# A fused transformer block: Q and K of the first two tiles read from the loaded weights on 32-column tiles, with the first stage re-ordered

## The chip, the cores and the metric

The kernel runs on one core of a Trainium2 chip. The metric is the device time of one execution in microseconds (us), taken over several runs. Five engines matter: TensorE (PE; PEld is its weight load), VectorE (DVE), ScalarE (ACT), GpSimd (POOL) and SyncE (SP), which issues the transfers. Each runs its own program in order, and they meet through semaphores.

## The reference

One block with adaptive layer norm over S = 2048 tokens, D = 448 channels, H = 16 heads of 28, F = 1792. Cut to what is computed:

```
mod = silu(c) @ w_mod                  # six rows of 448: sa, ca, ga, sb, cb, gb
h = layernorm(x) * (1 + ca) + sa
q, k, v = heads of h @ wqkv            # 448 -> 3 * 448
for each position s and head: keys at s - 2*w, w = 0..7, those >= 0
    o = softmax(q.k / sqrt(28)) @ v
x = x + ga * (o @ wo)
h = layernorm(x) * (1 + cb) + sb
x = x + gb * (gelu(h @ w1 + b1) @ w2 + b2)
```

Inputs and output are bf16.

## The kernel before

The dilation of 2 splits the tokens into two interleaved sub-sequences of 1024. A tile is 128 positions of both, so there are 8 tiles of 256 tokens. Attention runs in 9 batches of 114 positions: scores `lt` (L738), exp and a mask multiply into `et`, denominators `pd` (L760), outputs `po` (L771, 128 small matmuls of 64x57 a batch), a division, and the output projection `pw` (L803). The MLP (L548 and L554 for W1, L883 for W2) is done in two phases, each after its share of the batches, so that the chain of attention overlaps with W1 and W2 matmuls.

**Two ways to Q and K.** Tiles 0 and 1 take the short way: the normalised tokens `zy` are transposed on PE (`ptr`, L535), scaled and shifted into `hT`, and Q and K are made feature-major. Heads have 28 features but sit on 32 partitions of `qT` and `kT`, so the loaded weights `wqk_st` (128 rows) and `wqr_st` (the last 64 rows, kept twice, on both halves of the partitions) are first copied into `Wqk` and `Wqr` with every head spread to 32 columns: ten copies, lines L439 to L450. The matmuls (`pq`, L562, L548, L554) then take 128 spread columns as stationary weights and 128x256 of `hT` as moving data. Tiles 2 to 7 take the long way: `zy` goes through a DMA transpose `zT` (L527), DVE writes `hT` (L502), PE makes Q and K token-major with `hT` as the stationary side (L548, L554), and they come to `qT` and `kT` through ACT and DMA transposes (L631).

**What sets the order.** All work is recorded as numbered tasks; a written-out table `ORDER` gives the order in which they are emitted, an engine letter where a task has a choice of engine, and "+12@55" where 12 filler matmuls on zeros are put ahead (into the accumulator of task 55). `SLOTS` gives each buffer's place. The tables thus fix every engine's program. All transfers are issued by SP in table order; in the built program each waits also for the eighth transfer before it on SP.

**The first stage.** x and the weights of the first modulation (`wm_st`, `wm_r`), `wqk_st`, `wqr_st` and `Wv` are loaded; DVE takes layer-norm statistics (L456, L458), POOL or ACT turn them into `rs_all` (L469 on POOL), DVE writes `zy` (L478), whose tail columns are copied on POOL (L490). POOL also builds the attention mask (L280 to L289) and zero pads. silu(c) is made on DVE, L396, and copied to 32 columns on ACT, L398. The later modulation matrix `wmod` is loaded in four pieces (L362) for the matmuls of L641.

Of the kernel before, what the change touches and what calls it, by code (L numbers as in the profile page):

```python
# [10 lines left out]
BF16 = mybir.dt.bfloat16  # L11
# [55 lines left out]
487 401 490 454 403 402 436 453 455 370 444 404 434 371:D 456 372 491 457 488 405 459 493 458 460 445 492 435 494 461  # L67
# [3 lines left out]
513 515:D 547 599 516 564 602 481 568 569 570 604 571 603 546 605 572 548 606 573 628 607 608 574 549 635 575 550 609  # L71
612 636 577 630 578 637 610 629 576 640 579 638 581 639 611 613 580 582 583 641 631 586 633 587 651 584 614 632 585
616 588 615 617 642 618 648 646 647 621 654 634 619 645 622 652 620 656 649 623 644 658 643 625 624 650 589 590 626
591:A 664 655 627 653 439 657 592 659 556 665 662 663 674 666 660 661 669 667 675 668 678 676 679 677 686 672 673 671
687 681 670 680 690 691 694 697 693 682 688 692 685 695 683 689 701 684 698 696 709 699 710 702 711 712 705 700 703
706 704 707 708
# [77 lines left out]
def kernel(  # L154
# [41 lines left out]
    Wqk = cst.tile([128, KT - 1, 2, H, HP], BF16, name="Wqk")  # L196
    Wqr = cst.tile([128, 2, H // 2, HP], BF16, name="Wqr")
# [25 lines left out]
    silu_bf = cst.tile([128, KT], BF16, name="silu_bf")  # L223
# [11 lines left out]
    wqk_st = sb("hm", [128, KT - 1, 2 * D + HP - DH], BF16, "wqk_st")  # L235
    wqr_st = sb("h2", [128, 2 * D + HP - DH], BF16, "wqr_st")
# [9 lines left out]
    def dconst(us, fn, writes):  # L246
        early.append(add("DVE", us, fn, writes=writes, after=[one], name="const " + writes[0]))
# [22 lines left out]
    dconst(0.06, lambda: nc.vector.memset(neg_half[:], -0.5), ["neg_half"])  # L270
# [46 lines left out]
    def load(fn, us, writes, bufs=(), reads=(), fills=()):  # L317
        queue.append(add("SP", 0.5, fn, reads=reads, writes=writes, bufs=bufs, fills=fills, after=queue[-1:] if len(queue) < 4 else queue[3:4], xfer=us,
                         name="load " + writes[0]))
# [8 lines left out]
    def load_rest(a):  # L328
        load(lambda a=a: nc.sync.dma_start(out=wqr_st.t[KS * a:KS * a + KS, :], in_=A_wqkv[(KT - 1) * 128:D, 0:2 * D + HP - DH]),
             0.5, [f"wr{a}"], bufs=[wqr_st])  # L330

    def load_wv():
        load(lambda: nc.sync.dma_start(out=Wv[:, 0:KT - 1, :], in_=rows128(A_wqkv[0:(KT - 1) * 128, 2 * D:3 * D])), 1.15, ["wv"])
        for a in range(2):
            load(lambda a=a: nc.sync.dma_start(out=Wv[KS * a:KS * a + KS, KT - 1, :], in_=A_wqkv[(KT - 1) * 128:D, 2 * D:3 * D]),
                 0.2, [f"wvr{a}"])
# [17 lines left out]
    load_rest(0)  # L354
    load_rest(1)
    load_x(2, 4)
# [30 lines left out]
    def c_cols():  # L387
# [8 lines left out]
    add("DVE", 0.08, lambda: nc.vector.tensor_tensor(out=silu_bf[:], in0=e_c[:], in1=psc.t[:, 0, 0:128 * KT:128], op=ALU.mult),  # L396
        reads=["e_c"], bufs=[psc], writes=["silu"], name="silu")
    add("ACT", 0.18, lambda: nc.scalar.copy(out=silu_bc[:], in_=silu_bf[:].unsqueeze(2).to_broadcast([128, KT, HP])),  # L398
        reads=["silu"], writes=["silu_bc"], name="silu_bc")
# [32 lines left out]
    def spread(half):  # L432
        def heads(ap, h):
            return bass.AP(ap.tensor, ap.offset, [*ap.ap[:-1], [DH, h], [1, HP]])

        for ks in [[k] for k in range(KT - 1)]:
            k0, n = ks[0], len(ks)
            dst, src = (lambda k0=k0, n=n: Wqk[:, k0:k0 + n, half]), (lambda k0=k0, n=n: heads(wqk_st.t[:, k0:k0 + n, half * D:half * D + D], H))
            add("DVE", 0.06 + 0.18 * n, lambda dst=dst, src=src: nc.vector.tensor_copy(out=dst(), in_=src()), reads=[f"wqk{k}" for k in ks],  # L439
                bufs=[wqk_st], writes=[f"W{half}{k}" for k in ks], port=True, name="spread",  # L440
                alt={"ACT": (0.13 + 0.43 * n, lambda dst=dst, src=src: nc.scalar.copy(out=dst(), in_=src())),
                     "POOL": (0.1 + 0.5 * n, lambda dst=dst, src=src: nc.gpsimd.tensor_copy(out=dst(), in_=src()))})

        for a in range(2):
            rows, c0 = slice(KS * a, KS * a + KS), half * D + a * D // 2
            src = lambda rows=rows, c0=c0: heads(wqr_st.t[rows, c0:c0 + D // 2], H // 2)
            add("DVE", 0.22, lambda rows=rows, src=src: nc.vector.tensor_copy(out=Wqr[rows, half], in_=src()), reads=[f"wr{a}"],
                bufs=[wqr_st], writes=[f"Wr{half}{a}"], port=True, name="spread r",
                alt={"ACT": (0.33, lambda rows=rows, src=src: nc.scalar.copy(out=Wqr[rows, half], in_=src())),
                     "POOL": (0.4, lambda rows=rows, src=src: nc.gpsimd.tensor_copy(out=Wqr[rows, half], in_=src()))})  # L450


    exps, lt_mms, w1_mms, gelus = [], [], [], []

# [508 lines left out]
```

## Time and profile before

| quantity | value |
|---|---|
| median of 3 runs | 168.64 us (167.93 to 169.38) |
| the profiled execution: its own time | 169.75 us |
| its span on the core | 168.1 us |
| TensorE clock granted | 1.0 |
| PE busy | 161.5 us, 96% of the span, 2126 matmuls |
| DVE, ACT, POOL busy | 115.8, 102.7, 47.7 us |
| moved by DMA | 18.78 MB in 35574 packets |
| chain that ended last | PE 81%, DMA 10%, the rest 2% or less each |

The span is what the core's records cover; the execution's own time is 1.65 us longer. The median of the plain runs lies 1.1 us below the profiled execution's time. "Chain" is the work that ended last, followed back from the end. Up to about 34 us the chain runs through loads, DVE, POOL and transposes; from there on it is nearly all PE.

### The profile page before, as it was taken

The numbers are of one execution on the slowest core, as the hardware profiler recorded it, in microseconds if no ns is written. First come the engines' busy times: TensorE is split into PE (matmuls) and PEld (weight loads), VectorE is DVE, ScalarE is ACT, GpSimd is POOL, SyncE is SP. The second block draws the span as 40 slices with busy tenths as digits, with TensorE's granted clock in tenths as the row PEclk, the third lists the DMA queues.
The fourth block names the chain that finished last, engine by engine and source line by source line (L and its number), as shares of the span: only waits on it lengthen the run. The fifth ranks groups of instructions, "written<-read, shape, count | busy, mean of one in ns | idle before, by whom it ended". The sixth has DMA issues, their size and how long they took to land.

```text
span 168.1 us, 4962 instructions
## 1 busy us (share of the span) xinstructions
PE 161.5 (96%) x2126; PEld 83.4 (50%) x2126; DVE 115.8 (69%) x271; ACT 102.7 (61%) x142; POOL 47.7 (28%) x76
## 2 busy tenths in 40 slices
PE   7989989999997999999999999999999999999992
PEld 4768544345544544435565444556434455444562
DVE  6869899879899689998738877474798930400032
ACT  3368987779489954759866376956627730097300
POOL 4135252300361201269300113820003870007200
PEclk9999999999999999999999999999999999999999
DMA  5999989799997999910091000008110027110003
GB/s 153 325 335 297 168 265 134 152 201 170 221 200 182 236 150 236 169 35 0 4 139 46 4 0 0 4 0 97 35 55 0 0 43 195 49 60 0 0 0 109
DMA packets 35574, 18.78 MB, mean 112 GB/s; under 512 B 28508, under 2 KB 34593, under 8 KB 35553
## 3 DMA queue, kind: packets, MB, share of 16 engines
q1 hardware_dynamic: 35548, 18.47, 53.0%
q8 instruction: 16, 0.26, 0.7%
q14 instruction: 6, 0.04, 0.1%
q10 hardware_dynamic: 4, 0.00, 0.0%
HBM read 9.81 MB, written 1.84 MB: 69 GB/s over the span
## 4 chain that ended last, share of the span: by engine, by line
PE 81%; DMA 10%; DVE 2%; POOL 2%; issue 1%; SPq 1%; ACT 1%; POOLq 0%; DVEq 0%
PE p L883 26%; PE p L548 22%; PE pw L803 7%; PE pq L548 6%; PE p L554 4%; DMA x_all<-in_A_x_dram 4%; PE po L771 3%; PE lt L738 3%; PE pv L706 3%; PE pv L548 3%; DMA wm_st<-in_w_mod_dram 3%; DMA zT<-zy 2%; DMA kT<-zy 2%; PE pq L554 1%; PE pd L760 1%
## 5 line engine op out<-in xcount | busy, mean ns | idle before, releaser
L864 ACT ACTIVATE hm<-p,b_col 128x512 bf16<-128x512 f32 x56 | 33.9, 692 | 29.9 <-PE p L554 27.3
L883 PE MATMUL p<-w_s,hm 128*128 128x448 bf16 (+1 forms) x238 | 44.1, 342 | 0.0
L548 PE MATMUL p<-yT,w_s 128*128 128x512 bf16 x168 | 38.1, 379 | 0.0
L469 POOL TENSOR_TENSOR rs_all<-mvs,neg_half 128x2 f32<-128x2 f32 x22 | 16.7, 766 | 57.9 <-DVE mvs L458 57.8
L883 PEld LDWEIGHTS <-hm 128*128 128x128 bf16 x238 | 22.7, 98 | 19.2 <-issue 0.8
L889 DVE TENSOR_TENSOR x_all<-p,x1p 128x896 bf16<-128x896 f32 (+2 forms) x10 | 8.9, 902 | 25.9 <-PE p L883 25.9
L548 PEld LDWEIGHTS <-w_s 128*128 128x128 bf16 x168 | 15.8, 98 | 20.9 <-issue 2.9
L456 DVE BATCH_NORM_STATS2 stt<-x_all 128x6 f32<-128x448 bf16 x32 | 18.7, 610 | 1.2 <-DMA x_all<-in_A_x_dram 1.0
L745 ACT ACTIVATE et<-lt 128x928 bf16<-128x928 f32 x18 | 16.1, 947 | 5.3 <-PE lt L738 5.1
L841 POOL TENSOR_TENSOR x1p<-x_all,gbb_bc 128x448 f32<-128x448 bf16 x16 | 17.8, 1134 | 0.0
L548 PE MATMUL pq<-wqk_st,hT 128*128 128x448 bf16 x72 | 15.2, 354 | 0.6 <-DVE hT L502 0.5
L788 DVE TENSOR_TENSOR qT<-po,den 128x912 bf16<-128x912 f32 x9 | 9.9, 1104 | 7.0 <-ACT den L782 5.6
L751 DVE TENSOR_TENSOR et<-et,mask 128x928 bf16<-128x928 bf16 x18 | 11.6, 672 | 2.4 <-ACT et L745 2.4
L803 PE MATMUL pw<-wo_s,qT 128*128 128x448 bf16 x64 | 13.2, 353 | 0.0
L780 ACT ACTIVATE den<-pd 128x928 f32<-128x928 f32 x9 | 8.5, 940 | 5.8 <-PE pd L760 5.7
L819 DVE TENSOR_TENSOR h<-h,mod_bc 128x896 bf16<-128x896 bf16 x16 | 11.1, 709 | 0.3
L548 PEld LDWEIGHTS <-hT 128*128 128x128 bf16 x72 | 6.4, 98 | 7.7 <-issue 1.3
L628 ACT CAST zy<-pq 128x896 bf16<-128x896 f32 x10 | 9.0, 906 | 2.0 <-PE pq L554 1.9
L810 DVE TENSOR_TENSOR x_all<-pw,x_all 128x896 bf16<-128x896 f32 x8 | 8.7, 1088 | 1.7 <-PE pw L803 1.5
L782 ACT ACTIVATE den<-den,den_bias 128x928 f32<-128x928 f32 x9 | 9.6, 1072 | 0.2
L478 DVE TENSOR_SCALAR zy<-h,mvs,rs_all 128x448 bf16<-128x448 bf16 x16 | 6.6, 456 | 4.4 <-POOL rs_all L469 4.3
L456 DVE BATCH_NORM_STATS2 stt<-h 128x6 f32<-128x448 bf16 x16 | 9.4, 613 | 0.2
(115 smaller groups left out, 183.4 us busy)
## 6 DMA issues: line engine op xcount, KB each, us to landing
w_s<-in_B_w_dram SPq DMA_DIRECT2D x7, 224.0 KB, 4.2
out_dram<-x_all SPq DMA_DIRECT2D x7, 224.0 KB, 2.2
x_all<-in_A_x_dram SPq DMA_DIRECT2D x3, 448.0 KB, 6.0
wmod<-in_w_mod_dram SPq DMA_DIRECT2D x3, 448.0 KB, 7.0
w_s<-in_B_w_dram SPq DMA_DIRECT2D x3, 448.0 KB
wqk_st<-in_A_wqkv_dram SPq DMA_DIRECT2D x3, 225.0 KB
wm_st<-in_w_mod_dram SPq DMA_DIRECT2D x1, 672.0 KB
x_all<-in_A_x_dram SPq DMA_DIRECT2D x2, 224.0 KB, 2.6
```

The source lines that it names most:

```text
L456: add("DVE", 0.53, lambda: nc.vector.bn_stats(out=stt[:, w, b, 0:6], in_=src()), reads=reads, bufs=bufs, after=early if w == b == 0 else ( ...
L469: ways = {"POOL": (0.55 + 0.17 * n, lambda: nc.gpsimd.tensor_tensor(out=r, in0=v, in1=neg_half[:, 0:n], op=ALU.pow))}
L548: nc.tensor.matmul(out(), lhsT=lhs(kt, slice(0, 128)), rhs=rhs(kt, slice(0, 128)), start=first and kt == 0, stop=not first and kt == KT - 2)
L745: exps.append(add("ACT", 0.83, lambda half=half, lt=lt: nc.scalar.activation(out=et.t[:, 2 * half:2 * half + 2].rearrange("p r m c -> p r ...
L751: nc.vector.tensor_tensor(out=ev, in0=ev, in1=mask[:], op=ALU.mult)
L782: exps.append(add("ACT", 0.96, lambda: nc.scalar.activation(out=den.t[:], in_=den.t[:], func=ACT.Exp, scale=-1.0, bias=den_bias[:]), bufs= ...
L788: nc.vector.tensor_tensor(out=qT[:, :, LEAD + q00:LEAD + q00 + 2 * WQ], in0=po.t[:, :, 0:NS * 4 * WQ].rearrange("p j (m c) -> p m j c", c=WQ),
L803: nc.tensor.matmul(pw.t[:, s, 0:D], lhsT=qT[:, KT * s + ft, LEAD + 128 * p:LEAD + 128 * p + 128], rhs=wo_s[:, ft, :], start=(ft == 0), sto ...
L819: add("DVE", 0.55, lambda vec=vec, op=op: nc.vector.tensor_tensor(out=h2.t[:], in0=h2.t[:], in1=vec.unsqueeze(1).to_broadcast([128, NS, D] ...
L841: add("POOL", 1.0, lambda n=n: nc.gpsimd.tensor_tensor(out=x1p.t[:, n, :], in0=xn(p, n), in1=gbb2_bc[:], op=ALU.add), reads=[f"x{p}", "gbb ...
L864: gelus.append(add("ACT", 0.585, lambda f=f, a=a, p1=p1s[g]: nc.scalar.activation(out=hm.t[:, f].rearrange("p n c -> p (n c)"), in_=p1.t[: ...
L883: nc.tensor.matmul(p2.t[:, n, 0:c1 - c0], lhsT=hm.t[:, f, n, q * 128:(q + 1) * 128], rhs=w2_s[:, f, c0:c1], start=(f == parts[0][0]), stop ...
```

## The change

1. **Q and K of tiles 0 and 1.** A matmul now takes 32 columns of `wqk_st` or `wqr_st` (28 of a head and 4 of the next) as stationary weights and writes 32 partitions of the accumulator; the four column groups are filled by four matmuls in turn. The 64 matmuls on weights 128 columns wide become 256 on weights 32 wide (L565 of the changed file), with the same 128x256 of moving data each. The ten spread copies and `Wqk`, `Wqr` are gone. `ORDER` asks for 25 filler matmuls where it asked for 35. In all PE has 2308 matmuls for 2126.
2. **Loads.** `wqk_st` rows are 896 elements for 900; `wm_r`, `wqr_st` and the rest of `Wv` come in one transfer each onto 128 partitions where two on 64 did; tiles 2 and 3 of x come in a transfer each. The four pad columns of `wqk_st` and `wqr_st` are set to zero on DVE.
3. **silu** is written to 32 columns by one DVE operation; the ACT copy is gone.
4. **Order.** Tables, task numbers and SLOTS are new. From the scores matmul that starts at 33.71 us in the profile before, each engine's program is the same, instruction by instruction; only the first stage differs, and on PE everything after it stands 182 matmuls (364 instructions) later in the program.

On SP, in the first stage, `x_all`, `Wv` and `wmod` are loads and `zT` the transposes of tiles 2 and 3. Before:

```order
L339 DMA x_all<-in_A_x_dram 128x2x896 x2
L333 DMA Wv<-in_A_wqkv_dram 128x3x448
L335 DMA Wv<-in_A_wqkv_dram 64x448
L339 DMA x_all<-in_A_x_dram 128x2x896
L362 DMA wmod_274<-in_w_mod_dram 128x1792
L335 DMA Wv<-in_A_wqkv_dram 64x448
L362 DMA wmod_274<-in_w_mod_dram 64x1792
L527 DMA_TRANSPOSE zT<-zy_97 128x8x128
L527 DMA_TRANSPOSE zT<-zy_98 128x8x128
```

The same place in the changed kernel:

```order
L342 DMA x_all<-in_A_x_dram 128x896 x2
L338 DMA Wv<-in_A_wqkv_dram 128x3x448
L339 DMA Wv<-in_A_wqkv_dram 128x1x448
L342 DMA x_all<-in_A_x_dram 128x2x896 x2
L508 DMA_TRANSPOSE zT<-zy_96 128x8x128
L508 DMA_TRANSPOSE zT<-zy_97 128x8x128
L363 DMA wmod_581<-in_w_mod_dram 128x1792
L363 DMA wmod_581<-in_w_mod_dram 64x1792
```

The two `wmod` loads moved from ahead of the two transposes to behind them.

On POOL, in the first stage, `rs_all` is the inverse standard deviation and `zy` the copy of its tail columns. Before:

```order
L442 COPY Wqk<-wqk_st 128x512
L450 COPY Wqr<-wqr_st 64x256
L469 TENSOR_TENSOR rs_all<-mvs,neg_half 128x2
L450 COPY Wqr<-wqr_st 64x256
L469 TENSOR_TENSOR rs_all<-mvs,neg_half 128x2 x2
L280 MEMSET mask_90 128x58
L283 AFFINE_SELECT mask_90<-mask_90 64x58
L285 AFFINE_SELECT mask_90<-mask_90 64x58
L283 AFFINE_SELECT mask_90<-mask_90 64x58
L285 AFFINE_SELECT mask_90<-mask_90 64x58
L490 COPY zy_98<-zy_98 128x2x64
```

The same place in the changed kernel:

```order
L281 MEMSET mask_88 128x58
L284 AFFINE_SELECT mask_88<-mask_88 64x58
L286 AFFINE_SELECT mask_88<-mask_88 64x58
L284 AFFINE_SELECT mask_88<-mask_88 64x58
L286 AFFINE_SELECT mask_88<-mask_88 64x58
L290 COPY mask<-mask_88 128x928
L450 TENSOR_TENSOR rs_all<-mvs,neg_half 128x2 x4
L471 COPY zy_100<-zy_100 128x2x64
```

The copies of weights are gone, and the mask is built ahead of the first `rs_all`.

On PE, the end of the 128 outputs `po` of one attention batch and the matmuls behind them. Before, the first of these rows is the 1357th of the program:

```order
L771 LDWEIGHTS vb_115
L771 MATMUL po<-et,vb_115 32x57
L554 LDWEIGHTS hT
L554 MATMUL pq<-wqr_st,hT 128x448
L554 LDWEIGHTS hT
L554 MATMUL pq<-wqr_st,hT 128x448
L548 LDWEIGHTS hT
L548 MATMUL pq<-wqk_st,hT 128x448
```

In the changed kernel the first of them is the 1721st:

```order
L740 LDWEIGHTS vb_112
L740 MATMUL po<-et,vb_112 32x57
L535 LDWEIGHTS hT
L535 MATMUL pq<-wqr_st,hT 128x448
L535 LDWEIGHTS hT
L535 MATMUL pq<-wqr_st,hT 128x448
L529 LDWEIGHTS hT
L529 MATMUL pq<-wqk_st,hT 128x448
```

The instructions are the same and stand 364 places later.

The diff, cut to its core:

```diff
 ORDER = """
-3 14 17 0 1 15 5 9 10 18 11 16 13 19 20 2 6 24 21 73 55+12@55 26 12 71 25 56 72 74 57 75 22 58 77 23 59 60 27 62 61 76
+3 14 17 0 1 15 5 9 10 18 11 16 13 19 2 6 70 53+8@53 23 7 20 21 54 8 24 68 22 55 56 71 69 57 25 72 74 26 59 60+10@60 73
...
     def load_qk(kt):
-        load(lambda: nc.sync.dma_start(out=wqk_st.t[:, kt, :], in_=A_wqkv[kt * 128:kt * 128 + 128, 0:2 * D + HP - DH]), 0.62, [f"wqk{kt}"],
+        load(lambda: nc.sync.dma_start(out=wqk_st.t[:, kt, 0:2 * D], in_=A_wqkv[kt * 128:kt * 128 + 128, 0:2 * D]), 0.62, [f"wqk{kt}"],
              bufs=[wqk_st])
...
+    def both(src, n):
+
+        return bass.AP(src.tensor, src.offset, [[n, 2], *src.ap])
+
+    def load_rest():
+        load(lambda: nc.sync.dma_start(out=wqr_st.t[:, 0:2 * D], in_=both(A_wqkv[(KT - 1) * 128:D, 0:2 * D], 0)),
+             0.5, ["wr0", "wr1"], bufs=[wqr_st])
...
-    add("ACT", 0.18, lambda: nc.scalar.copy(out=silu_bc[:], in_=silu_bf[:].unsqueeze(2).to_broadcast([128, KT, HP])),
-        reads=["silu"], writes=["silu_bc"], name="silu_bc")
+    add("DVE", 0.2, lambda: nc.vector.tensor_tensor(
+        out=silu_bc[:], in0=e_c[:].unsqueeze(2).to_broadcast([128, KT, HP]),
+        in1=psc.t[:, 0, :].rearrange("p (k n) -> p k n", n=128)[:, :, 0:HP], op=ALU.mult),
+        reads=["e_c"], bufs=[psc], writes=["silu_bc"], name="silu_bc")
...
-    def spread(half):
...
+                        rest, first = kt == KT - 1, not state
+                        state.append(kt)
+                        for r, a in [(r, a) for r in range(4) for a in range(2)] if rest else [(r, a) for a in range(2) for r in range(4)]:
+                            rows = slice(KS * a, KS * a + KS) if rest else slice(0, 128)
+                            w = wqr_st.t[rows] if rest else wqk_st.t[:, kt]
+                            d0 = half * D + DH * (4 * (i + 2 * a) + r)
+                            nc.tensor.matmul(pq.t[HP * r:HP * r + HP, a, NS * 128 * i:NS * 128 * (i + 1)], lhsT=w[:, d0:d0 + HP],
+                                             rhs=hT[rows, NS * kt:NS * kt + NS, c0:c0 + 128], start=first, stop=len(state) == KT,
+                                             tile_position=(rows.start, HP * r))
```

More of the change, by code (lines that the diff above doesn't have):

```diff
@@ L244, with dconst @@
     early = []
-    def dconst(us, fn, writes):
-        early.append(add("DVE", us, fn, writes=writes, after=[one], name="const " + writes[0]))
+    def dconst(us, fn, writes, bufs=()):
+        early.append(add("DVE", us, fn, writes=writes, bufs=bufs, after=[one], name="const " + writes[0]))
     def const(us, fn, writes, reads=()):
@@ L317, in load @@
     def load(fn, us, writes, bufs=(), reads=(), fills=()):
-        queue.append(add("SP", 0.5, fn, reads=reads, writes=writes, bufs=bufs, fills=fills, after=queue[-1:] if len(queue) < 4 else queue[3:4], xfer=us,
+        queue.append(add("SP", 0.5, fn, reads=reads, writes=writes, bufs=bufs, fills=fills, after=queue[-1:] if len(queue) < 3 else queue[2:3], xfer=us,
                          name="load " + writes[0]))
@@ L324, in load_qk @@
     def load_qk(kt):
[L325 removed]
+        load(lambda: nc.sync.dma_start(out=wqk_st.t[:, kt, 0:2 * D], in_=A_wqkv[kt * 128:kt * 128 + 128, 0:2 * D]), 0.62, [f"wqk{kt}"],
              bufs=[wqk_st])
[L328 to L330 removed]
+    def both(src, n):
[3 more added lines that the diff above has]
+             0.5, ["wr0", "wr1"], bufs=[wqr_st])
     def load_wv():
         load(lambda: nc.sync.dma_start(out=Wv[:, 0:KT - 1, :], in_=rows128(A_wqkv[0:(KT - 1) * 128, 2 * D:3 * D])), 1.15, ["wv"])
[L334 to L336 removed]
+        load(lambda: nc.sync.dma_start(out=Wv[:, KT - 1, :], in_=both(A_wqkv[(KT - 1) * 128:D, 2 * D:3 * D], 0)), 0.3, ["wvr0", "wvr1"])
     def load_x(p0, p1):
@@ L347 @@
          2.1, ["wm0"], bufs=[wm_st])
-    for v in range(2):
-        load(lambda v=v: nc.sync.dma_start(out=wm_r.t[KS * v:KS * v + KS, :], in_=w_mod[(KT - 1) * 128:D, v * D:v * D + D]),
-             0.25, [f"wmr{v}"], bufs=[wm_r])
+    load(lambda: nc.sync.dma_start(out=wm_r.t[:], in_=both(w_mod[(KT - 1) * 128:D, 0:D], D)), 0.4, ["wmr0", "wmr1"], bufs=[wm_r])
     for kt in range(KT - 1):
@@ L353 @@
     load_x(1, 2)
-    load_rest(0)
-    load_rest(1)
-    load_x(2, 4)
+    load_rest()
+    load_x(2, 3)
+    load_x(3, 4)
     load_wv()
@@ L430 @@
     modulation()
-    def spread(half):
[L433 to L450, printed above, removed]
     exps, lt_mms, w1_mms, gelus = [], [], [], []
     def stats(src, w, b, reads, bufs=()):
-        add("DVE", 0.53, lambda: nc.vector.bn_stats(out=stt[:, w, b, 0:6], in_=src()), reads=reads, bufs=bufs, after=early if w == b == 0 else (),
+        add("DVE", 0.53, lambda: nc.vector.bn_stats(out=stt[:, w, b, 0:6], in_=src()), reads=reads, bufs=bufs,
             writes=[f"st{w}_{b}"], name="stats")
@@ L541, in front_ln, with summed @@
             affine(u, lambda kt: ptr[kt % 2].t[:, :, kt // 2], [(ptr[0], q) for q in range(np_)], ptr, True)
-    def summed(items, slot, reads, bufs, fills, name, after=(), split=None):
+    def summed(items, slot, reads, bufs, fills, name, after=()):
         def full(first):
@@ L555, in rest @@
                                  tile_position=(rows.start, 0))
-        us = 3.5 * len(items) * slot + 0.1
-        if split:
-            for kt in range(KT - 1):
-                def piece(kt=kt):
-                    for out, lhs, rhs in items:
-                        nc.tensor.matmul(out(), lhsT=lhs(kt, slice(0, 128)), rhs=rhs(kt, slice(0, 128)), start=kt == 0, stop=False)
-                add("PE", len(items) * slot, piece, reads=reads + [f"W{name[-2]}{kt}", f"h{kt}_0"], bufs=bufs, fills=fills, after=after,
-                    instr=2 * len(items), name=f"{name}f{kt}")
-            return [add("PE", 0.5 * len(items) * slot, lambda: rest(False), reads=reads + split, bufs=bufs, fills=fills, mode="64x128",
-                       instr=2 * len(items), name=name + "r")]
         both = dict(reads=reads, bufs=bufs, joins=fills, after=after)
@@ L576, in summed, with front_qk @@
                 add("PE", 0.5 * len(items) * slot, lambda: part(rest), instr=2 * len(items), mode="64x128", name=name + "r", **both)]
[L578 to L582 removed]
+    def front_qk(p):
+        c0 = LEAD + 128 * p
         for half in range(2):
[L585 to L611 removed]
@@ new lines, in front_qk, with piece @@
+            pq = psum("pq")
+            done = []
+            for i in range(2):
+                state = []
+                def piece(kts, i=i, half=half, pq=pq, state=state):
+                    for kt in kts:
+                        rest, first = kt == KT - 1, not state
[7 more added lines that the diff above has]
+                                             tile_position=(rows.start, HP * r))
+                mine = []
+                for kts in [[kt] for kt in range(KT - 1)] if p == i == 0 else [list(range(KT - 1))]:
+                    mine.append(add("PE", 0.22 * len(kts), lambda kts=kts, piece=piece: piece(kts), reads=["wqpad"] + [f"wqk{kt}" for kt in kts] + [f"h{kt}_{p}" for kt in kts],
+                                    bufs=[pq, wqk_st], joins=[pq], after=done, mode="128x32", instr=16 * len(kts),
+                                    name=f"qk{p}_{half}{'ab'[i]}f" + (str(kts[0]) if len(kts) == 1 else "")))
+                mine.append(add("PE", 0.11, lambda piece=piece: piece([KT - 1]), reads=["wqpad", "wr0", "wr1", f"h{KT - 1}_{p}"],
+                                bufs=[pq, wqr_st], joins=[pq], after=done, mode="64x32", instr=16, name=f"qk{p}_{half}{'ab'[i]}r"))
+                done = mine
@@ L614, in natural_qk @@
+            dst = (kT if half else qT)[:, :, c0:c0 + 128].rearrange("p (s f) c -> p s f c", s=NS)
+            src = lambda pq=pq: pq.t[:].rearrange("p a (i s c) -> p s (a i) c", i=2, s=NS)
+            add("ACT", 0.91, lambda dst=dst, src=src: nc.scalar.copy(out=dst, in_=src()), bufs=[pq], writes=[f"{'qk'[half]}{ft}_{p}" for ft in range(4)],
+                alt={"DVE": (1.14, lambda dst=dst, src=src: nc.vector.tensor_copy(out=dst, in_=src()))}, name="evac_qk")
     def natural_qk(p):
@@ L897 @@
         front_ln(u, True)
-        if k == 0 and u[0] not in NATURAL:
-            spread(0)
-            spread(1)
         if u[0] in NATURAL:
@@ L903 @@
         else:
-            front_qk(u)
+            front_qk(u[0])
     b1_cols()
```

83 lines of the change are left out of this document (28 added, 55 removed), and 21 rows, old and new, of tables (ORDER, SLOTS).

## The prediction

> **What bounds the kernel now.** I read the head of the page first, for how much of the span PE is at work.
>
> ```profile
> span 168.1 us, 4962 instructions
> PE 161.5 (96%) x2126; PEld 83.4 (50%) x2126; DVE 115.8 (69%) x271; ACT 102.7 (61%) x142; POOL 47.7 (28%) x76
> q8 instruction: 16, 0.26, 0.7%
> ```
>
> PE has work in 96% of the span, so a stage can save only what PE idles there, or PE's own work. The third line is the queue that brings instructions: 0.26 MB in 16 packets, 16 KB each. PE's 2126 matmuls and as many weight loads make 4252 instructions, and 4252 / 16 = 266; what each packet holds comes out below. Next, the waits of PE, with total, count and longest:
>
> ```profile
> PE lt L738 <- issue: 0.8, 1, 0.8
> PE pq L548 <- DVE hT L502: 0.5, 1, 0.5
> PE pq L562 <- DVE Wqk L439: 0.4, 1, 0.4
> PE lt L738 <- DMA kT<-zy: 0.4, 1, 0.4
> ```
>
> Three of the four belong to the first stage, 1.3 us together. The longest, "issue", is waited for by no semaphore. The chain of waits shows where these lie (start, length, what):
>
> ```profile
> 6.32 6.00 DMA x_all<-in_A_x_dram
> ...
> 15.87 0.07 POOL mask L280
> ...
> 17.17 0.29 POOL zy L490
> ...
> 17.56 3.38 DMA zT<-zy
> ...
> 22.79 2.25 PE pq L548 x11
> ...
> 30.57 3.09 DMA kT<-zy
> ...
> 33.71 0.70 PE lt L738 x62
> ...
> 50.57 0.48 PE lt L738 x43
> 51.05 0.85 issue
> 51.90 0.34 PE lt L738 x18
> ...
> 57.52 0.02 issue
> 57.55 0.62 PE po L771 x58
> ```
>
> Up to 22.79 us the chain runs from a load of x over statistics, POOL and the transpose to the first token-major Q and K. From there PE hardly stops: the two "issue" pieces fall in the middle of one run of like matmuls. I counted PE's matmuls up to each of them, and up to four other moments (window, length, busy time and count of PE, PEld, DVE, ACT, POOL, clock, DMA share, GB/s):
>
> ```profile
> 0.00:11.60 11.60, 9.82 (x95) 7.17 (x96) 9.21 (x50) 5.01 (x11) 3.98 (x18) 1.00 0.84 264
> 0.00:37.69 37.69, 34.96 (x551) 20.73 (x559) 31.45 (x106) 26.33 (x39) 12.18 (x33) 1.00 0.92 226
> 0.00:38.20 38.20, 35.47 (x610) 21.19 (x610) 31.69 (x106) 26.84 (x40) 12.18 (x33) 1.00 0.91 224
> 0.00:45.03 45.03, 42.30 (x735) 24.85 (x738) 37.87 (x115) 31.50 (x45) 13.22 (x34) 1.00 0.94 220
> 0.00:51.50 51.50, 48.33 (x861) 27.80 (x862) 44.16 (x131) 37.05 (x52) 16.02 (x37) 1.00 0.98 214
> 0.00:57.54 57.54, 53.95 (x989) 30.61 (x990) 49.50 (x144) 42.64 (x59) 17.47 (x39) 1.00 1.01 217
> 0.00:85.32 85.32, 81.72 (x1316) 43.76 (x1324) 73.92 (x193) 61.08 (x83) 28.22 (x51) 1.00 0.87 181
> 0.00:85.95 85.95, 82.35 (x1390) 44.34 (x1390) 73.92 (x193) 61.38 (x84) 28.22 (x51) 1.00 0.87 181
> ```
>
> The pieces stand at matmuls 861 and 989: 128 matmuls and 128 weight loads apart, which is 256 instructions. Sixteen KB for 256 instructions is 64 bytes each. So I read the pieces as ends of an instruction block, with ends at every 128th matmul: ..., 93, 221, ..., 605, 733, 861, 989, ..., 1373, 1501. Views of the DMA queues over three short windows, 39.6 to 40.7, 49.44 to 50.67 and 87.5 to 88.46 us, hold one packet of that queue each:
>
> ```profile
> q8 instruction: 1, 0.02, 5.4%
> q8 instruction: 1, 0.02, 6.1%
> q8 instruction: 1, 0.02, 6.0%
> ```
>
> A packet that fills one of 16 engines' time would read 6.2%, so each took nearly its whole window. Matmul 605 is passed just before 38.20 (x610), 733 just before 45.03 (x735), 1373 between 85.32 and 85.95: each packet follows one passage, and the packet of 49.44 came after PE had entered the block before the stall at 51.05. A block's successor is fetched when the block is entered. From entry to landing that is about 2.5 us (38.2 to 40.7), 2.6 (85.85 to 88.46) and 5.6 (45.0 to 50.67). In the third case PE went on only at 51.90, 1.2 us after the packet. A block that PE runs through faster than this cannot have its successor ready.
>
> **The shift of the blocks.** PE's program after 33.71 us is the same, 182 matmuls later. So a block end of the changed kernel at matmul 861 is old matmul 679, and the block from 733 to 861 holds the old 551 to 679. The rows say what that is: 551 matmuls are begun at 37.69 us, and then come these:
>
> ```profile
> 37.70 1.44 PE L771 MATMUL po<-et,vb 64*32 64x57 bf16 x128
> 85.33 1.39 PE L771 MATMUL po<-et,vb 64*32 64x57 bf16 x128
> ```
>
> The block is exactly the 128 `po`, gone through in 1.4 us; in the old program the end at 605 cuts them in two. A later block, from 1501 to 1629, is old 1319 to 1447: the second row, with 1316 begun at 85.32. Each must then wait for its successor. With 2.55 us from entry to landing (the two cases nearest in place) and 0.6 for the step from packet to work, halfway between none and the 1.2 measured once, that is 2.55 + 0.6 - 1.4 = 1.75 us at about 39, and 1.75 again at about 87. Without the step each is 1.15, with all of it 2.35. PE has nothing to hide it with: no other wait of it after 33.71 us stands in the list but the one at 51.05. That one goes, since the block that ends in it moves: -0.85. What takes its place as late there? Nothing in the list of waits. Sum behind the first stage: 3.5 - 0.85 = +2.65, with bounds 2.3 - 0.85 = +1.45 and 4.7 - 0.85 = +3.85.
>
> [...]
>
> **The first stage.** Its end is the `lt` at 33.71. From 22.79 to there PE's only idle is 0.4 for `kT`, and the transfer of `kT` itself is issued behind work of that same stretch, so I take the whole stretch to move with the start of 22.79. That start has two conditions.
>
> The transposes: POOL's mask work stands between the `rs_all` and the `zy` copy, 15.87 to 17.17, 1.3 us of the chain, and it now lies ahead of all `rs_all`, when POOL has room (3.98 us of work in the first 11.60). The load at 6.32 is split, and its first half has a shorter transfer. The two loads of `wmod` that stood ahead of the transposes on SP stand behind them. So `zT` should land at least 1.3 us sooner, at about 19.6 instead of 20.94 (17.56 + 3.38). The queue allows it:
>
> ```profile
> 16.00:17.00 1.00, 1.00 (x40) 0.88 (x33) 1.00 (x4) 0.65 (x1) 0.81 (x4) 1.00 0.36 97
> ```
>
> Its DMA share fell to 0.36 while POOL was at the mask. What is put behind the transposes, `wmod`, is used by L641 at 27 us (row below), so it has room.
>
> PE: it was free 0.5 us ahead of 22.79, that is at 22.25. Its wait of 0.4 for `Wqk` goes with the copies, and ten fillers of the size of an old QK matmul (0.12, below) go (-1.2), of which I count half, since some stood in waits. The price of the new matmuls comes from these rows, with mean durations in ns behind the bar in the first two:
>
> ```profile
> L641 PE MATMUL pb<-wmod,silu_bc 128*32 128x448 bf16 (+1 forms) x16 | 1.1, 357 | 0.0
> L641 PEld LDWEIGHTS <-silu_bc 128*32 128x32 bf16 (+1 forms) x16 | 0.3, 94 | 0.8 <-issue 0.7
> 27.03 1.05 PE L641 MATMUL pb<-wmod,silu_bc 128*32 128x448 bf16 x16
> 75.21 3.19 PE L883 MATMUL p<-w_s,hm 128*128 128x448 bf16 x16
> 12.58 2.79 PE L548 MATMUL pq<-hT,Wqk 128*128 128x256 bf16 x24
> 15.31 0.61 PE L554 MATMUL pq<-hT,Wqr 64*128 64x256 bf16 x8
> ```
>
> Sixteen matmuls on 32-column weights take 1.05 us, sixteen full ones of the same 448 columns 3.19: four run beside one another. The first row's last matmul begins 1.05 - 0.36 = 0.69 after the first, in 3.75 rounds: 0.18 a round, against (3.19 - 0.36) / 15 = 0.19 for a full one. So a round of four costs what one full matmul costs, and weight loads of 0.09 are hidden. An old QK matmul has 2.79 / 24 = 0.12 us, and the half-row ones run in pairs: eight in 0.61 us. The old form needs 48 + 16 / 2 = 56 such times for both tiles. The new form needs, per group of eight heads, 3 x 2 rounds of 128 rows and one of 64 rows (eight matmuls on halves of the rows): 7, and with two tiles, two halves and two groups 56 as well. The matmuls come out even, 56 x 0.12 = 6.7 us: 0, or +1.0 if each of eight changes between 128 and 64 rows costs a matmul's time. The copies were on DVE, ACT and POOL beside PE; without them these engines only come earlier.
>
> Against this stands the block that QK itself fills. In the profile matmul 93 is passed at about 11.6 us (x95), and the next packet is in this view of 14.9 to 16.2:
>
> ```profile
> q8 instruction: 1, 0.02, 5.4%
> ```
>
> That is 4.6 us. In the changed kernel matmul 93 is QK's 24th, at about 9.9 us, and 221 follows some 4 us later, as 100 of the 128 run four at a time. So 0.6 to 1.8 us of stall falls into QK. PE at the token-major Q and K: 22.25 - 0.4 - 0.6 + 1.0 = 22.25, bounds 21.1 and 23.9. Against 22.79 that is -0.5, bounds -1.2 (where `zT` takes over) and +1.1.
>
> [...]
>
> **Sum.** -0.5 + 2.65 = +2.15. The profiled execution took 169.75 us with its span of 168.1 and 1.65 around it; the changed one should have a span of 170.25 and 171.9. The median of the runs, 168.64, lies 1.1 below the profiled one, so **170.8 us** on the median.
>
> **Rivals.**
>
> *No stall at the blocks.* If the successor of a short block is there in time, because more than one block is fetched ahead, both +1.75 go: -0.5 - 0.85 = -1.35, 167.3 us, faster. If the 0.85 was no block end either, it stays: 168.1. For it: the 256 instructions of 51.90 to 57.5 passed their end with 0.02 us of idle. Against it: the two pieces exactly 128 matmuls apart. [...] It decides if entry to landing falls under 1.4 us; the shortest I saw is 2.5. Chance 0.29.
>
> *Fetches as late as at 45 us.* If they take 5.6 us while the queue is full (share 0.92 up to 37.69), the first stall is 5.6 - 1.4 = 4.2 and 1.75 for the second: +5.95 - 0.85 - 0.5 = +4.6, 173.2 us. Chance 0.08.
>
> *Weight loads of column tiles in the open.* 48 x 0.09 = 4.3 us in QK, which PE hands on to 33.71: 168.64 + 4.3 + 2.15 = 175.1. Against it L641. Chance 0.04.
>
> *QK as forecast, but a first stage that gains nothing* since `kT` still lands at 33.66: in the range of the forecast.
>
> **Numbers.** Forecast 0.59. A measurement of this kernel can tell about 1% from no change, 1.7 us: 166.95 and 170.33 are the limits. The forecast's own range is 168.64 - 1.2 + 1.45 = 168.9 to 168.64 + 1.1 + 3.85 = 173.6, both ends unlikely together; I take 169.3 to 172.6. Above 170.33 lies about 0.55 of it (0.33), the rest is within 1% (0.26). Of the first rival 0.13 is faster and 0.16 within; the second and third are slower (0.12). Together: faster 0.13, same 0.42, slower 0.45. The range goes from 167.0, which leaves out 0.1 of the first rival, to 172.8, which leaves out the rest.
>
> **What would show it.** Right: a gap of over 1 us in PE without a semaphore just behind each of the two `po` runs of 128 (near 39 and 87 us), each shortly behind a packet of the instruction queue; none near 51; a smaller one in QK; `zT` landed by about 19.6 us; four QK matmuls in 0.11 us. Wrong: no gap behind `po`; a `kT` that lands after 34 us; QK rounds of 0.2 us.

## The result and the profile after

The changed kernel takes 183.49 us (median of four runs, 182.06 to 185.06), the kernel before 169.01 in the same comparison: a ratio of 1.083, 95% interval 1.073 to 1.093. It is slower by some 14 us; the forecast was 170.8 with a range of 167.0 to 172.8. The profiled execution of the changed kernel is the longest of the four, 185.06 us with a span of 183.3, and the ratio leaves it out as a slow run; the other three have a median of 182.21. Its mean granted clock is 0.981 and theirs are 0.962 to 0.981, so the lower clock seen below is not peculiar to it.

The head of the page and the line of the instruction queue:

```profile
span 183.3 us, 5310 instructions
PE 168.1 (92%) x2308; PEld 85.6 (47%) x2308; DVE 116.5 (64%) x270; ACT 101.1 (55%) x141; POOL 44.1 (24%) x70
q8 instruction: 18, 0.29, 0.7%
```

PE is idle 15.2 us where it was idle 6.6, and it is also 6.6 us longer at work, although it has ten fillers fewer. So there are two kinds of loss: waits, and matmuls that run longer. PE's waits (total, count, longest):

```profile
PE pq L565 <- DMA wqr_st<-in_A_wqkv_dram: 2.6, 1, 2.6
PE ps_col L411 <- DVE wm_d L419: 2.4, 1, 2.4
PE lt L707 <- issue: 2.1, 1, 2.1
PE pq L535 <- issue: 1.7, 1, 1.7
...
PE pd L729 <- issue: 1.2, 1, 1.2
PE p L529 <- DMA yT<-zy: 0.7, 1, 0.7
```

The two largest are loads of the first stage (`wm_d` is made from `wm_r`). Three are "issue", of which the forecast named two, behind `po`. The chain of waits places them (start, length, what):

```profile
3.89 11.03 DMA wqr_st<-in_A_wqkv_dram
14.93 0.04 issue
14.97 1.39 PE pq L565 x24
...
28.91 0.52 PE lt L707 x48
29.43 2.11 issue
31.54 0.42 PE lt L707 x14
...
43.90 0.63 PE lt L707 x62
...
48.01 1.21 PE po L740 x128
49.21 0.29 PE pq L535
49.50 1.74 issue
51.25 0.35 PE pq L535
...
100.17 0.37 PE pd L729 x2
100.54 1.21 issue
```

The `lt` that stood at 33.71 us stands at 43.90: 10.2 of the 15.2 us of span are lost in the first stage. Behind it 183.3 - 43.9 = 139.4 us follow, where 168.1 - 33.71 = 134.4 followed: 5.0. Windows of PE (count of matmuls begun, granted clock, DMA share and GB/s at the end of the row):

```profile
12.30:14.90 2.60, 0.11 (x4) 0.00 (x0) 0.00 (x0) 0.00 (x0) 0.00 (x0) 1.00 0.13 49
0.00:31.00 31.00, 23.18 (x479) 14.87 (x479) 20.92 (x83) 13.15 (x23) 6.92 (x24) 1.00 0.75 209
31.90:34.80 2.90, 2.90 (x22) 1.01 (x18) 1.79 (x5) 1.96 (x3) 0.39 (x1) 0.50 0.91 58
0.00:51.00 51.00, 41.14 (x862) 23.55 (x863) 34.62 (x109) 27.75 (x42) 9.04 (x27) 0.97 0.76 175
51.60:55.30 3.70, 3.70 (x12) 1.48 (x13) 1.03 (x2) 1.75 (x3) 1.04 (x1) 0.54 1.07 159
0.00:101.00 101.00, 89.69 (x1628) 47.10 (x1629) 74.71 (x192) 61.15 (x84) 24.56 (x45) 0.97 0.73 154
```

Three things are to be seen. In the first row every engine waits, and the DMA engines are busy to 0.13, which is the share of two of sixteen (0.125). The three "issue" stalls fall at matmuls 479, 862 and 1628, which are block ends by the forecast's count of 93 and every 128th (477, 861, 1629). And behind the first two stalls the granted clock is 0.50 over 2.9 us and 0.54 over 3.7 us, which by my estimate lengthens PE's work by half of 2.9 and 0.46 x 3.7 us: 3.2 of the 6.6 us.

Most of the other part lies earlier. The first row counts PE up to the `lt` at 43.90 in the changed kernel, the second up to the same `lt` at 33.71 in the kernel before:

```profile
0.00:43.90 43.90, 35.54 (x651) 20.34 (x655) 29.21 (x99) 21.48 (x34) 8.35 (x26) 0.96 0.72 177
0.00:33.71 33.71, 30.98 (x462) 18.79 (x462) 28.43 (x101) 23.12 (x35) 12.18 (x33) 1.00 0.90 229
```

Of the 10.2 us, 5.6 are waits of PE (8.4 for 2.7) and 4.6 are longer work. Only about 1.5 of the 4.6 is the half clock behind the stall at 29.43. The rest looks like work at a lower rate between 9 and 18 us. Eight transposes on PE, behind the wait for `wqr_st`, take 1.03 us in the changed kernel (first row) and 0.61 in the kernel before (second row).

```profile
16.30 1.03 PE L516 MATMUL ptr<-ident,zy 128*128 128x128 bf16 x8
11.28 0.61 PE L535 MATMUL ptr<-ident,zy 128*128 128x128 bf16 x8
```

The clock column of this profile reads 1.00 there. In the run below with the same joined loads and 74 matmuls more, the eight transposes take the same 1.03 us, and the clock is recorded at half:

```profile
9.10:18.10 9.00, 6.24 (x105) 4.42 (x105) 4.76 (x16) 1.82 (x4) 0.70 (x1) 0.50 0.66 210
```

That the changed kernel had the same clock there is inferred from these lengths. With the loads split, below, these eight take 0.62 us, so the lower rate there goes with the late loads; the eight before them take 1.01 in both, so not all of it does.

### The profile page after: what moved, and what is told of

It reads as the page before. It is cut to its first block, busy times and chain, and to the rows that moved or that the text cites. A ratio compares the mean times of both kernels' runs of the same rounds, so it can differ in the third digit from the quotient of the medians.

```text
span 183.3 us, 5310 instructions
## 1 busy us (share of the span) xinstructions
PE 168.1 (92%) x2308; PEld 85.6 (47%) x2308; DVE 116.5 (64%) x270; ACT 101.1 (55%) x141; POOL 44.1 (24%) x70
## 4 chain that ended last, share of the span: by engine, by line
PE 83%; DMA 9%; issue 4%; SPq 2%; DVE 1%; ACT 1%; POOL 0%; DVEq 0%; ACTq 0%
PE p L852 24%; PE p L529 20%; PE pq L529 8%; DMA wqr_st<-in_A_wqkv_dram 6%; PE pw L772 5%; PE pq L565 5%; PE pv L675 5%; PE p L535 4%; PE lt L707 3%; DMA yT<-zy 3%; PE po L740 2%; PE pq L535 2%; PE pd L729 2%; PE pv L529 1%; PE ptr L516 1%
## 5 line engine op out<-in xcount | busy, mean ns | idle before, releaser
L450 POOL TENSOR_TENSOR rs_all<-mvs,neg_half 128x2 f32<-128x2 f32 x21 | 15.8, 758 | 76.5 <-DVE mvs L439 76.5
L529 PE MATMUL pq<-wqk_st,hT 128*128 128x448 bf16 x72 | 15.8, 367 | 0.0
L772 PE MATMUL pw<-wo_s,qT 128*128 128x448 bf16 x64 | 14.1, 371 | 0.0
L772 PEld LDWEIGHTS <-qT 128*128 128x128 bf16 x64 | 6.3, 103 | 7.0 <-issue 2.0
L597 ACT CAST zy<-pq 128x896 bf16<-128x896 f32 x8 | 7.1, 915 | 4.5 <-PE pq L535 3.3
```

Source lines behind the costliest of these rows:

```text
L450: ways = {"POOL": (0.55 + 0.17 * n, lambda: nc.gpsimd.tensor_tensor(out=r, in0=v, in1=neg_half[:, 0:n], op=ALU.pow))}
L529: nc.tensor.matmul(out(), lhsT=lhs(kt, slice(0, 128)), rhs=rhs(kt, slice(0, 128)), start=first and kt == 0, stop=not first and kt == KT - 2)
L772: nc.tensor.matmul(pw.t[:, s, 0:D], lhsT=qT[:, KT * s + ft, LEAD + 128 * p:LEAD + 128 * p + 128], rhs=wo_s[:, ft, :], start=(ft == 0), sto ...
```

## The experiments

Three causes are to be told apart: the joined loads (J), the blocks of instructions (R), and the column tiles or the new order themselves. Each step below was compared with the kernel before on the same chip; the ratio is to that kernel, with its 95% interval.

**Joined loads taken apart.**

```diff
-        load(lambda: nc.sync.dma_start(out=wqr_st.t[:, 0:2 * D], in_=both(A_wqkv[(KT - 1) * 128:D, 0:2 * D], 0)),
+        load(lambda: [nc.sync.dma_start(out=wqr_st.t[KS * a:KS * a + KS, 0:2 * D], in_=A_wqkv[(KT - 1) * 128:D, 0:2 * D]) for a in range(2)],
```

and the same for `wm_r` and the rest of `Wv`.

> The changed kernel, but with the three joined loads (wm_r, wqr_st, the rest of Wv) issued as two transfers of 64 partitions each again. Theory J (the joined transfers run on two of the sixteen DMA engines, so they and everything queued behind them on those two land late): wqr_st lands by 10 us instead of 14.93, the wait of 2.6 for it and that of 2.4 for wm_d are gone, and the scores matmul that stands at 33.71 us in the kernel before comes at 33 to 35 us instead of 43.9. The rest, 139.4 us in the changed kernel, stays: 172 to 175 us in all. Rival (the column tiles or the new order of the first stage are slow): no better than 180.

Measured: 178.48 us, ratio 1.051 (1.041 to 1.061): 5.0 below the changed kernel, less than J asked. The `lt` of 43.90 comes at 39.26, where J had 33 to 35. The waits for `wqr_st` are gone and that for `wm_d` is 0.5. Windows of this run, the first over the time in which the changed kernel stood still, the others up to its stalls:

```profile
12.30:14.90 2.60, 2.60 (x101) 2.15 (x104) 1.91 (x8) 2.27 (x6) 0.70 (x1) 1.00 0.81 281
0.00:15.90 15.90, 13.63 (x223) 8.88 (x223) 13.14 (x61) 6.19 (x14) 5.26 (x22) 1.00 0.82 254
0.00:20.00 20.00, 16.94 (x351) 11.43 (x351) 16.71 (x70) 8.54 (x16) 5.26 (x22) 1.00 0.85 225
0.00:26.50 26.50, 21.02 (x479) 13.67 (x479) 21.34 (x85) 13.38 (x23) 6.90 (x24) 1.00 0.89 244
```

With the loads in time, PE gets to QK earlier and runs into block ends there: it stops at matmuls 223, 351 and 479, three block ends in a row (221, 349, 477). PE's waits of this run name them "issue":

```profile
PE lt L709 <- issue: 3.4, 2, 2.4
...
PE pq L567 <- issue: 0.6, 1, 0.6
```

That is 4.0 us in the first stage, of which the changed kernel shows only the last, 2.1. The third stall has a stretch of lower clock behind it, 0.65 from 27.00 to 31.50. Both are part of why the gain fell short. A window from where PE goes on after the second stall to where it goes on after the third:

```profile
20.37:26.84 6.47, 4.09 (x129) 2.25 (x129) 4.98 (x16) 4.47 (x8) 1.64 (x2) 1.00 0.92 286
```

PE enters the block at its start and goes on behind it 6.5 us later, with the DMA engines busy to 0.92. The timeline of the same run has QK matmuls in between:

```profile
16.09 0.62 PE L567 MATMUL pq<-hT,wqk_st 128*32 128x256 bf16 x16 [0.56 <-issue]
```

Sixteen in 0.62 us with the tail of the last: the four rounds that the forecast counted, at its price. The column tiles themselves are not slow here.

**One of the three loads alone taken apart**, `wqr_st`; the diff is the one line above.

> The changed kernel with wqr_st alone split in two transfers; wm_r and the rest of Wv stay joined. If wqr_st is what costs, it is as fast as the split loads, 178 to 179 us. If each joined load costs by its rows on two DMA engines, wm_r still lands near 8.2 us instead of 6.5, with a wait of about 2.4 us ahead of the modulation, and the time is between, 180 to 182 us.

Measured: 180.88 us, ratio 1.066 (1.060 to 1.073), between the changed kernel and the split loads. Taking `wqr_st` apart is worth 2.6 us, the other two together 2.4. PE waits 3.1 us for `wm_d` here. So `wqr_st` costs, and so do the other two together; these two were not told apart, and the runs of this kernel lie between 179.41 and 183.76.

**Joined loads in the kernel before.** The first of two loads of each pair is issued as the joined one, the second not at all.

```diff
-        load(lambda a=a: nc.sync.dma_start(out=wqr_st.t[KS * a:KS * a + KS, :], in_=A_wqkv[(KT - 1) * 128:D, 0:2 * D + HP - DH]),
+        load(lambda a=a: None if a else nc.sync.dma_start(out=wqr_st.t[:], in_=both(A_wqkv[(KT - 1) * 128:D, 0:2 * D + HP - DH], 0)),
```

> The kernel before with wm_r, wqr_st and the rest of Wv loaded in one transfer each onto 128 partitions, as in the changed kernel; nothing else altered. Theory J: wqr_st lands 5 us later or more, and the scores matmul of 33.71 us comes 6 to 10 us later: 175 to 179 us. Rival: within 1 us of the kernel before.

Measured: 177.08 us against 169.65, ratio 1.041 (1.033 to 1.049). This edit alone costs 7.4 us, with the old QK and the old order. PE's waits:

```profile
PE pq L566 <- DVE Wqk L443: 3.8, 2, 3.1
PE ps_col L414 <- DMA wm_r<-in_w_mod_dram: 2.1, 1, 2.1
```

`Wqk` is copied from `wqk_st`, whose loads landed 6.5 to 10.0 us after their issue here. `wqr_st` lands at 15.42 us and the `lt` of 33.71 comes at 41.40, 7.7 later. So J holds in both kernels. A window up to that `lt` shows how the 7.7 us come about:

```profile
0.00:41.40 41.40, 34.26 (x462) 20.60 (x462) 28.89 (x102) 23.27 (x35) 12.14 (x33) 0.88 0.77 189
```

The same 462 matmuls took 30.98 us in the kernel before. So 3.3 us are PE's slower work at a mean clock of 0.88 (0.50 from 16.00 to 20.00), and 4.4 are waits. The late loads thus cost twice in this run; in the kernel before the clock reads 1.00 from 16.00 to 20.00.

**The block ends moved in the kernel before.** Eighteen fillers of 256 columns become four of 64 each: 54 matmuls more, of the same streamed length.

```diff
-        for _ in range(n):
-            nc.tensor.matmul(t.sums[0].t[:, 0, 0:256], lhsT=warm_w[:, 0:128], rhs=warm_w[:, 0:256], start=True, stop=True)
+        for _ in range(n):
+            k = 1 + min(3, shift[0])
+            shift[0] -= k - 1
+            for j in range(k):
+                m = 128 if k == 1 else 32
+                w = 256 // k if k != 3 else 85
+                nc.tensor.matmul(t.sums[0].t[0:m, 0, 0:w], lhsT=warm_w[:, 0:m], rhs=warm_w[:, 0:w], start=True, stop=True)
```

with `shift` starting at 54.

> The kernel before with 54 matmuls more: 18 of its fillers are each cut in four, so that its blocks of 256 instructions end as in the changed kernel, before and behind each run of 128 po. Nothing else is altered. Theory R: a stall of 1.2 to 2.4 us just behind po near 39 and near 87 us, the first of them with a stretch of half clock behind it (about 1.5 us more), the one near 51 gone: 171 to 174 us. Rival: within 0.7 us of the kernel before.

Measured: 174.69 us, ratio 1.028 (1.019 to 1.037): 5.0 us. The cut fillers themselves cost little, since the `lt` of 33.71 comes at 33.92; what follows is the same program with its block ends in other places. PE's timeline about the two runs of `po`, with the idle time ahead in brackets:

```profile
37.91 1.41 PE L778 MATMUL po<-et,vb 64*32 64x57 bf16 x128
39.26 0.36 PE L561 MATMUL pq<-wqr_st,hT 64*128 64x448 bf16 x2
41.51 1.31 PE L555 MATMUL pq<-wqk_st,hT 128*128 128x448 bf16 x6 [1.89 <-issue]
...
86.90 1.53 PE L778 MATMUL po<-et,vb 64*32 64x57 bf16 x128
88.25 0.38 PE L767 MATMUL pd<-et,ones_k 64*32 64x464 bf16 x3
90.08 0.38 PE L767 MATMUL pd<-et,ones_k 64*32 64x464 bf16 x5 [1.45 <-issue]
```

From the start of the block to going on are 41.51 - 37.91 = 3.6 and 90.08 - 86.90 = 3.2 us. The forecast had 2.55 + 0.6 = 3.15. The stall of 51 us is gone from this run's waits; one of 0.44 is new, at matmul 1117, a block end too. A window behind the second stall:

```profile
90.90:93.80 2.90, 2.90 (x9) 1.20 (x8) 0.00 (x0) 2.85 (x3) 0.00 (x0) 0.50 0.02 6
```

The half clock came here behind the second stall, not, as I expected, behind the first: from 41.50 to 45.00 the clock is 1.00.

**The block ends moved back, with split loads.** The same edit of the filler in the kernel with split loads, with 74 matmuls more (24 fillers in four, one in three).

> The split loads and 74 matmuls more in PE's program: 24 fillers of 256 columns are each cut in four of 64, one in three, so that the blocks of 256 instructions end where they end in the kernel before, relative to the matmuls behind the first stage. Theory R (an instruction block that is run through faster than its successor is fetched stalls PE): the stalls just behind the two runs of 128 po are gone, the one inside lt near 51 is back with 1.0, and the half clock after the first of them is gone: 3 to 5 us below the split loads alone, 167 to 170 us. Rival (the stalls belong to something else near po): they stay where they are, within 1 us of the split loads alone.

Measured: 172.26 us, ratio 1.012 (1.003 to 1.021), 6.2 below the split loads. The stalls behind `po` are gone. That is more than the 3 to 5 expected, and the other theory is out. Of the gain, 2.2 us lie ahead of the `lt` that came at 39.26 and now comes at 37.05. The stall inside `lt` that was expected back with 1.0 didn't come: PE passes that block end without a wait. One stall of 1.3 us remains at matmul 479 in the first stage, and the time is still 2 us above the upper end of 170.

**The same with 51 more.**

> The split loads with 51 matmuls more in the place of 74, by cutting fillers in the same way. Theory R, with 5 us from entry to going on while the DMA queue is full and 4 us later, from the times of the run with 74: the stall of 1.5 us at the 479th matmul becomes two of 0.9 and 0.7 us, the others stay small, and the time is 170 to 172 us. Were the stalls not bound to the block ends, it would be that of the run with 74 within 0.5 us, with the stall at the same work.

Measured: 172.47 us, ratio 1.020 (1.015 to 1.024). The stall at matmul 479 isn't there, nor are the two of 0.9 and 0.7 us that were expected in its place; one of 0.5 stands at matmul 862, and PE waits for `kT`, `vb` and `wm_st` some 1 us each. The stall didn't stay at its work, which speaks for block ends, but their size was not forecast, and the time alone says nothing against the run with 74.

**The block ends moved back, with joined loads.** The filler edit with 74 in the changed kernel.

> The changed kernel with its joined loads, and 74 matmuls more by cutting fillers, as in the run with split loads and 74 more: blocks end where they end in the kernel before, relative to the matmuls behind the first stage. If the two causes are separate and add up, it gains on the changed kernel what the same step gained on the split loads, about 6 us, most of it by the stalls at the 862nd and 1628th matmul and the half clock behind the first: 176 to 179 us, with wqr_st still landing near 15 us. If the late loads hide part of the stalls of the first stage, it gains less, 3 to 5 us: 179 to 181.

Measured: 177.16 us, ratio 1.049 (1.042 to 1.055): 6.3 below the changed kernel, where the split loads gained 6.2 by the same step. Joined or split makes 4.9 us here and 5.0 there. The two causes add up within the spread of the runs, and the time is in the first of the two expectations. The stalls behind `po` are gone; the half clock of the first stage, shown above, stays.

**A quarter of the QK instructions.** Q and K of tiles 0 and 1 by 64 matmuls on 128 neighbouring columns in the place of 256 on 32, split loads, and ten matmuls more by cut fillers.

```diff
-                        for r, a in [(r, a) for r in range(4) for a in range(2)] if rest else [(r, a) for a in range(2) for r in range(4)]:
+                        for r, a in [(0, 0), (0, 1)]:
...
-                            nc.tensor.matmul(pq.t[HP * r:HP * r + HP, a, NS * 128 * i:NS * 128 * (i + 1)], lhsT=w[:, d0:d0 + HP],
+                            nc.tensor.matmul(pq.t[:, a, NS * 128 * i:NS * 128 * (i + 1)], lhsT=w[:, d0:d0 + 128],
```

> The changed kernel with the split loads, but Q and K of tiles 0 and 1 made by 64 matmuls with 128 neighbouring columns of the loaded weights each, in the place of 256 with 32: the same streams of 256 columns, so the same PE time, with a quarter of the instructions. The heads don't come to their places, so the features of Q and K of these two tiles are not those of the reference; the work behind them is unaltered. Ten matmuls are added by cutting fillers, so that the program has as many PE instructions as the kernel before and its blocks end at the same matmuls behind the first stage. Theory I (the number of instructions in QK is what the split loads left over, through the fetch of blocks): the stalls of 0.7, 1.1 and 2.5 us in QK and the first lt are gone, and the time is 166 to 169 us. Rival (the order of loads and of the first stage is itself slower): 171 to 173 us, as with the split loads and 74 more matmuls.

Measured: 170.10 us, ratio 1.006 (1.002 to 1.009): 2.2 below the split loads with 74 more, and 0.9 above the kernel before. Against the run with 51 more, on the same chip, it is 2.4, and the two intervals don't meet. It falls between the two expectations. The stalls in QK are gone, as theory I has it. Not all of the gain is shown to come from that: QK starts at 9.04 us for 10.07 with 74 more, and the seven fillers ahead of it take 0.94 us, where seven took 1.68 with the split loads. One stall of 0.8 us, named "issue", is left at matmul 974, inside `po`. That is no block end by the forecast's count (861, 989), and its cause stays open. The order of the first stage gains nothing. The chain of waits and PE's timeline of this run:

```profile
30.16 3.31 DMA kT<-zy
33.47 0.04 issue
33.52 0.70 PE lt L716 x62
```

```profile
27.78 0.37 PE L619 MATMUL pb<-wmod,silu_bc 128*32 128x448 bf16 x4 [0.74 <-DMA wmod<-in_w_mod_dram]
```

The `lt` comes at 33.52 instead of 33.71. The `zT` transposes landed at 18.9 us in this run, 2.0 sooner than in the kernel before. What they gained was given back to `wmod`, which now stands behind them, and to `kT`, which landed 0.2 sooner. In this run the chain to `kT` goes through a later load of x (9.56 to 15.83 us), its statistics and a later `zT`.

**An attempt to do better than both.** In the kernel before, each two neighbouring fillers become one of 512 columns, 16 matmuls fewer, which takes the block end near 51 us out of `lt`.

```diff
-        for _ in range(n):
-            nc.tensor.matmul(t.sums[0].t[:, 0, 0:256], lhsT=warm_w[:, 0:128], rhs=warm_w[:, 0:256], start=True, stop=True)
+        w = [512] * (n // 2) + [256] * (n % 2)
+        for m in w:
+            nc.tensor.matmul(t.sums[0].t[:, 0, 0:m], lhsT=warm_w[:, 0:128], rhs=warm_w[:, 0:m], start=True, stop=True)
```

> The kernel before with every two of its neighbouring fillers of 256 columns made one of 512: 16 PE matmuls fewer, the same filler time. Theory R: the block end that stalls near 51 us moves by 16 matmuls into the matmuls of pv behind, and the block becomes longer; that stall of 1.0 us is gone or shorter, and no block is faster than 4.3 us: 167.3 to 168.8 us, 0.4 to 1 us below the kernel before. Rival: no difference, the 1.0 us stays in the middle of lt.

Measured: 169.91 us, ratio 1.002 (0.998 to 1.006), no difference. The stall near 51 is gone, but another one took its place:

```profile
37.14 0.80 PE L772 MATMUL po<-et,vb 64*32 64x57 bf16 x72
39.03 0.61 PE L772 MATMUL po<-et,vb 64*32 64x57 bf16 x56 [1.09 <-issue]
```

This is the block end at 605. It stood inside `po` before as well, without a stall; in the kernel before with joined loads, at the same instruction, it has one of 0.64 us. So whether such a block's successor is there in time isn't settled by the program alone. I found no version faster than the kernel before.

## Why the prediction was wrong

By medians, the 14 us come apart like this:

| step | us | difference | ratio to the kernel before |
|---|---|---|---|
| changed kernel | 183.49 | | 1.083 |
| joined loads split | 178.48 | -5.0 | 1.051 |
| 74 matmuls more, block ends moved | 172.26 | -6.2 | 1.012 |
| a quarter of the QK instructions | 170.10 | -2.2 | 1.006 |
| kernel before (beside that run) | 169.16 | -0.9 | 1 |

The first two steps are clear in both columns. The third compares two chips; by the ratios it is 0.6%, about 1 us, with intervals that overlap, and by the run with 51 more on the same chip it is 2.4 us. The forecast was for a slower kernel, and it is slower; but two thirds of the loss stand in the first stage, where the forecast had a gain.

**The first stage, "-0.5, bounds -1.2 and +1.1".** This is the step that failed: it measured +10.2, of which 5.6 us are waits of PE and 4.6 its longer work. The prediction listed the split of x and the move of `wmod`, and never priced the joining of `wm_r`, `wqr_st` and `Wv`, though front and diff show it. That omission is the larger part, 5.0 us by the split loads and 7.4 in the kernel before. The sum also put nothing for a lower clock, which followed these waits and is 3.3 us of the 7.7 in the kernel before with joined loads. The trace of before held no row of such a transfer; the window of 12.30 to 14.90 in the changed kernel shows DMA at 0.13, the share of two engines of sixteen. The source of the joined load begins with a dimension of 2, and the two numbers agree; that the one comes from the other is my inference. I didn't weigh that dimension, and so had no rival of this kind; the only sign of a late load that I had listed was a late `kT`. The sign of `zT` landed by 19.6 failed: the second one is issued at 21.5 us and lands at 25.7.

The second part of the failure is the block stall in QK. The prediction had 0.6 to 1.8 us, at one block end. (Its sum takes 1.0, which isn't the middle of that range, and its bounds 21.1 and 23.9 follow from no terms that it names.) With the loads in time there are three in a row, in QK and the first `lt`, with 4.0 us. A form that needs four times the instructions for the same stream comes to block ends four times as often, and I followed only the first of them.

**The blocks behind the first stage, "+2.65, bounds +1.45 and +3.85".** Mechanism and places were right: stalls behind both runs of 128 `po`, none near 51. The two waits are 1.7 and 1.2 by the list of waits, for 1.75 each. The whole stretch came out at +5.0 and outside its bounds, by what followed the stalls: the clock of 0.54 from 51.60 to 55.30 costs an estimated 0.46 x 3.7 = 1.7 us, and a wait of 0.7 for `yT` came up; some 0.5 us are not traced. The first rival ("no stall at the blocks"), for which I had 0.29, is out: where the block ends were moved, the stalls moved with them. Of 22 "issue" stalls of PE in the eleven profiles, 21 stand within two matmuls of a block end; the other is the one at matmul 974. That a late fetch is what PE waits for is inferred from this and from the packets: in the changed kernel PE enters the block of `po` at 47.82 us, and one packet begins between 48.7 and 48.8 and takes 0.783 x 16 x 0.1 = 1.25 us (the queue reads 78.3% of 16 engines over that 0.1 us), so that it ends about 1.2 us before PE goes on at 51.25. In the kernel before, the shift by 54 matmuls alone costs 5.0 us.

**Column tiles.** Forecast right where PE ran at its full rate: rounds of four at one full matmul's time, no open weight loads. The third rival is out: with split loads sixteen matmuls pass in 0.62 us, where the rival had 0.09 us more for each of their four rounds.

**The second rival**, fetches as late as 5.6 us behind `po`, is out as well: 3.4 us from 47.82 to 51.25 in the changed kernel's timeline, for the forecast's 3.15. A delay as long did show elsewhere, in the first stage: 6.5 us from 20.37 to 26.84 with split loads, with DMA at 0.92.

**The move of `zT` and the mask.** `zT` did land sooner once the loads were split and QK was short (18.9 us for 19.6 forecast), but the sentence "so it has room", on `wmod`, was wrong by 0.7 us, and "I take the whole stretch to move with the start of 22.79" was wrong: `kT` has its own chain through SP. What remains of 0.9 us against the kernel before isn't taken apart.

## What to carry to other kernels

Count instructions as well as streams: here PE ran through the 256 instructions of 128 `po` in 1.4 us and went on only 3.2 to 3.6 us after it had entered them, in the first stage up to 6.5 us after, and an edit of the first stage moved such places to the middle of the kernel (stalls of 1.7 and 1.2 us). Look at the outermost dimension of every transfer that is joined or broadcast: three loads with a 2 there made the kernel before 7.4 us slower. Price every item of a change, also the one that looks like tidying, and compare the front of a changed program by when each load has landed.

## What the runs showed of the hardware

While the changed kernel waited for `wqr_st`, whose source has an outermost dimension of 2, the DMA share was 0.13, that of two engines of sixteen, at 49 GB/s: issued at 3.89 us, it landed 11.03 us later, where the second of its two loads in the kernel before landed 4.5 us after its issue. No run tried a dimension between this 2 and the 64 rows of the split loads. A load issued behind it came late too: of `wqk_st`, the part issued at 4.49 us landed 11.0 us after its issue, that of 3.42, ahead of `wqr_st`, 6.5 us. The stalls of PE of 2.11 us at 29.43 and of 1.74 at 49.50 were followed by a lower clock, 0.50 in the window of 31.90 to 34.80 and 0.54 in that of 51.60 to 55.30. Not every stall was: in the kernel before with moved ends the clock was 0.50 behind the stall of 1.45 us and 1.00 behind that of 1.89. Around the waits for loads it was 0.50 as well, from 9.10 to 18.10 with joined loads and 74 matmuls more. Why a stall is followed by the lower clock in one place and not in another was not shown.
